# A decode layer's first weight load in two transfers, and x's transfers behind ScalarE's first function table

## The chip, the cores and the metric

The kernel runs on one core of one Trainium2 chip. The core has five engines with instruction queues of their own: PE (TensorE, matrix products), DVE (VectorE), ACT (ScalarE), POOL (GpSimd) and SP (SyncE, which here only issues transfers). Sixteen DMA engines move data between the device memory (HBM) and the core's on-chip memory (SBUF, 128 partitions). PE writes its results to a second memory, PSUM. The metric is the time of one execution in microseconds on the device; lower is better. A time that is given as a median is over runs without the profiler's page; the profile is of one further execution.

## The reference

One token of a transformer layer with attention and a gated feed-forward part side by side, all in float32:

```python
x = A_x                                   # 1 x 1 x 1024
xn = _layernorm(x, axis=-1)
return x + _A_ref(xn, A_k_cache, A_v_cache, A_wq, A_wo) + _B_ref(xn, B_w_gate, B_w_up, B_w_down)

# _A_ref: 32 query heads, 4 key heads, the last 4096 of 65536 cached positions, head size 128
q = (x @ wq)                              # wq 1024 x 4096
k, v = the last 4096 rows of k_cache, v_cache, each shared by 8 query heads
p = softmax(q k^T * 128 ** -0.5);  o = p v;  return o @ wo      # wo 4096 x 1024

# _B_ref
h = gelu(x @ w_gate) * (x @ w_up)         # 1024 x 3584 each
return h @ w_down                         # 3584 x 1024
```

With one token nearly all of the work is to read the weights and the cached window once: 94 MB.

## The kernel before, in words

Everything large goes through one buffer in SBUF, `ring`, of 128 partitions by 32768 float32 values. A list, `PLAN`, says in which order the pieces of weights and cache come, at which column of the ring each begins, and which earlier piece has to be used up before it may be loaded: two loads of wq (`("q", 0)` at column 0 and `("q", 1)` at 16384) may start at once, then keys and values of two pairs of heads, the two halves of w_gate, w_up, wo and w_down take their turns in the halves and quarters of the ring. `load` issues the transfers of one piece, all of them on SyncE's queue; `used` issues what waits for a piece, after the code that uses it. So SyncE's queue has the loads in the order of `PLAN`, and each waits there until its place in the ring is free.

The piece `("q", 0)` is 512 rows of wq, four rows to each partition: 64 KB, without a gap, in each of 128 partitions (partition p takes rows 4p to 4p + 3). Before the change `load` moves it in one transfer of 128 partitions. Keys are moved in two transfers of 64 partitions each, to the even and to the odd ones; all other pieces in transfers of 128 partitions.

The start of the program is in this order. ScalarE issues two transfers that bring x, cut into two rows of 512, to `x_rows` (one row a transfer), and two that bring x into `x_out`, which is added to the result at the end. VectorE clears or fills the constant tiles; one of them is `avg`, a tile of 128 x 128 values 1/1024. GpSimd makes `ident`, the identity. Then `used(None)` issues the two loads of wq on SyncE, which has nothing in front of them. `layer_norm` turns `x_rows` into columns with four transposes on PE, gets mean and variance with two products by `avg`, takes a square root on ScalarE (`AF.Sqrt`; right behind it a dummy `AF.Exp` of one column, so that the next function table is loaded early), and writes the normalized x to `xz`.

`project` multiplies a piece of weights with `xz`: of each partition's four rows, two go to PE (32 products of 128 x 512 for a piece of wq) and two to VectorE, which scales a row by a value for each partition and adds it to `part`; `projected` adds VectorE's part to PE's sum at the end. The work on a piece waits for the landing of all its transfers.

The order of all instructions is that of the program text. The class `Flow` records each instruction's reads and writes, builds the program twice, and in the second pass adds just those waits that the reads and writes ask for. All instructions pass through one line of `Flow.issue`, so the profile names line 208 for nearly everything, and groups are told apart by their tiles.

Of the kernel before, what the change touches and what calls it, by code (L numbers as in the profile page):

```python
# [5 lines left out]
F32 = mybir.dt.float32  # L6
AF = mybir.ActivationFunctionType
# [4 lines left out]
P = 128  # L12
D = 1024
# [5 lines left out]
NR = 4  # L19
NJ = D // (NR * P)  # L20
# [217 lines left out]
RING = 32768  # L238
# [11 lines left out]
def decode_layer(nc, x, k_cache, v_cache, wq, wo, w_gate, w_up, w_down, out):  # L250
    consts = stream = work = Pool(nc.nc, "sbuf")
    psum = Pool(nc.nc, "psum")

    def fours(w, jj):
        return w[NR * P * jj:NR * P * (jj + 1), :].rearrange("(p r) n -> p r n", r=NR)


    def windows(cache, i):
        pair = cache[0, 2 * i:2 * i + 2, SK - WIN:, :]
        return pair.rearrange("g (p j) d -> p g (j d)", p=P // 2)  # L260


    def grouped(w, start, rows):
        return w[start:start + P * rows, :].rearrange("(p t) n -> p t n", p=P)


    def sources(kind, i):
        if kind == "q":
            return [fours(wq, i)]
        if kind == "g":  # L270
            return [fours(w_gate, i)]
        if kind == "u":
            return [fours(w_up, i)]
        if kind == "ua":
            return [fours(w_up, i)[:, :2]]
        if kind == "ub":
            return [fours(w_up, i)[:, 2:]]
        if kind in "kv":
            cache = k_cache if kind == "k" else v_cache
            return [windows(cache, i)]  # L280
        if kind == "o":
            return [grouped(wo, P * WIDE * i, WIDE)]
        return [grouped(w_down, P * GROUP * i, min(GROUP, TD - GROUP * i))]

    ring = stream.tile([P, RING], F32, name="ring")
    loaded = {}

    def load(key, at):

        parts = {("d", 2): 2, ("d", 3): 4}.get(key, 1)  # L290
        first = at
        if key[0] in "kv":

            dst = ring[:, at:at + RING // 4]
            if key[0] == "v":
                nc.sync.dma_start(dst, sources(*key)[0])
            else:
                for odd in range(2):
                    nc.sync.dma_start(dst[odd:P:2], sources(*key)[0][:, odd])
            loaded[key] = ring[:, at:at + RING // 4]  # L300
            return
        for src in sources(*key):
            rows, n = src.shape[1:]
            dst = ring[:, at:at + rows * n].rearrange("p (t n) -> p t n", n=n)
            at += rows * n
            step = rows // parts
            for t in range(0, rows, step):
                cuts = 2 if key == ("d", 3) and t == rows - 1 else 1
                for cut in range(cuts):
                    cols = slice(cut * n // cuts, (cut + 1) * n // cuts)  # L310
                    nc.sync.dma_start(dst[:, t:t + step, cols], src[:, t:t + step, cols])
        loaded[key] = ring[:, first:at]

    def used(key):

        for new, at, old in PLAN:
            if old == key:
                load(new, at)


    x_rows = work.tile([NJ, NR * P], F32, name="x_rows")
    x_in = x.rearrange("a b (j p) -> (a b j) p", j=NJ)
    for j in range(NJ):
        nc.scalar.dma_start(x_rows[j:j + 1, :], x_in[j:j + 1, :])
    x_out = work.tile([P, CO], F32, name="x_out")
    nc.vector.memset(x_out, 0.0)
    x_in = x.rearrange("a b (h c n) -> (a b c) h n", h=2, c=4)
# [8 lines left out]
        out=ident, in_=ident, compare_op=ALU.not_equal, fill=1.0, base=0,  # L336
        pattern=[[-1, P]], channel_multiplier=1,
    )
    avg = consts.tile([P, P], F32, name="avg")
    nc.vector.memset(avg, 1.0 / D)  # L340

    xz = consts.tile([P, NR, NJ, 32], F32, name="xz")
    nc.vector.memset(xz, 0.0)
# [429 lines left out]
```

## Time and profile before

| | |
|---|---|
| median of 3 runs | 227.65 us (227.53 to 227.72) |
| profiled execution, its own time | 227.77 us |
| its span, first to last instruction | 225.9 us |
| busy: PE / DVE / ACT / POOL | 117.4 / 107.2 / 28.0 / 0.7 us |
| read from HBM | 94.38 MB, 418 GB/s over the span |
| issue to landing, two loads of wq | 21.9 and 40.8 us |

A row of the timeline gives the start in us, the duration in us, the engine, the line, the operation, the tile written `<-` the tiles read, the shape, and how many instructions it merges; in brackets stands how long the engine had been idle before it and what ended that. SPq and ACTq are the issuing of transfers on SyncE's and ScalarE's queues: the duration of such a row is that of issuing, not of moving data. "DMA to landing" is the time from an issue to the moment at which all of its data is there. In the windows, the DMA share is the mean busy share of the 16 DMA engines; a piece of a transfer is counted in the window in which it starts, so short windows can show more than 1. The chain of waits is followed back from the last instruction, at each step to what released it.

### The profile page before, as it was taken

What the parts mean: (1) busy time and instruction counts of PE and PEld (TensorE: products, weight loads), DVE (VectorE), ACT (ScalarE), POOL (GpSimd) and SP (SyncE); (2) the same over time, 40 slices, a digit from 0 to 9 for tenths busy, and PEclk for the clock granted to TensorE, in tenths of its full rate; (3) what the DMA queues carried; (4) which work ended last, traced back from release to release, by engine and by line L of the source; (5) the groups of instructions that cost most, each with busy time, mean ns of one, the idle gap of its engine ahead of it and who ended that gap; (6) DMA issues with size and microseconds to landing.
All of it is one profiled execution on the core that took longest, in us unless ns stands there. A gap on an engine that the chain in (4) does not pass through costs nothing.

```text
span 225.9 us, 2481 instructions
## 1 busy us (share of the span) xinstructions
PE 117.4 (52%) x1107; PEld 58.4 (26%) x1107; DVE 107.2 (47%) x129; ACT 28.0 (12%) x54; POOL 0.7 (0%) x6
## 2 busy tenths in 40 slices
PE   0120900558799861999844662135309905561756
PEld 0010200113655621755611110010004902220322
DVE  7030920591236082236059589149209705993801
ACT  2020000002435400455400310000000000000000
POOL 1000000000000000000000000000000000000000
PEclk9999995587999998599979958559956955855888
DMA  9899899899999999998999998999999999999992
GB/s 372 372 418 511 371 418 511 354 412 438 437 487 428 387 412 438 429 505 376 429 404 426 447 503 366 447 455 464 386 441 464 395 444 395 435 418 412 432 394 108
DMA packets 3242, 94.53 MB, mean 418 GB/s; under 512 B 398, under 2 KB 414, under 8 KB 1056
## 3 DMA queue, kind: packets, MB, share of 16 engines
q1 hardware_dynamic: 3208, 94.38, 97.4%
q8 instruction: 8, 0.13, 0.2%
q14 instruction: 2, 0.02, 0.0%
q10 hardware_dynamic: 24, 0.01, 0.0%
HBM read 94.38 MB, written 0.00 MB: 418 GB/s over the span
## 4 chain that ended last, share of the span: by engine, by line
DMA 80%; DVE 16%; PE 2%; issue 0%; SPq 0%; DVEq 0%
DMA ring<-in_B_w_gate 26%; DMA ring<-in_A_wq 18%; DVE part L208 14%; DMA ring<-in_A_wo 14%; DMA ring<-in_B_w_up 11%; DMA ring<-in_B_w_down 11%; DVE out_part L208 2%; PE out L208 2%; DVE y L208 0%; SPq L208 0%; DVE y_last L208 0%; DVEq L86 0%; DVE d L208 0%
## 5 line engine op out<-in xcount | busy, mean ns | idle before, releaser
L208 PE MATMUL acc<-ring,xz 128*32 128x512 f32 x176 | 31.7, 825 | 39.2 <-DMA ring<-in_A_wq 22.9
L208 DVE SCALAR_TENSOR_TENSOR part<-ring,xz,part 128x3584 f32<-128x3584 f32 (+1 forms) x9 | 37.2, 4128 | 21.8 <-DMA ring<-in_A_wq 12.5
L208 PE MATMUL tp<-ident,ring 128*128 128x128 f32 x128 | 20.6, 311 | 8.8 <-DMA ring<-in_A_k_cache 6.0
L208 DVE SCALAR_TENSOR_TENSOR out_part<-ring,oz,out_part 128x1024 f32<-128x1024 f32 x15 | 19.3, 1285 | 8.1 <-DMA ring<-in_A_wo 7.6
L208 PEld LDWEIGHTS acc<-ring,xz 128*32 128x32 f32 x176 | 7.1, 142 | 59.5 <-issue 25.2
L208 PE MATMUL out<-ring,hz 128*32 128x256 f32 (+1 forms) x160 | 13.9, 515 | 13.7 <-DMA ring<-in_B_w_down 13.7
L208 PE MATMUL out<-ring,oz 128*32 128x256 f32 x128 | 11.8, 551 | 17.3 <-DMA ring<-in_A_wo 17.3
L208 PEld LDWEIGHTS tp<-ident,ring 128*128 128x128 f32 x128 | 15.5, 156 | 16.9 <-DMA ring<-in_A_k_cache 6.9
L208 DVE COPY kT<-tp 128x512 f32<-128x512 f32 x12 | 8.1, 690 | 20.0 <-PE tp L208 20.0
L208 ACT ACTIVATE kT<-tp 128x512 f32<-128x512 f32 x20 | 11.4, 596 | 26.9 <-PE tp L208 26.9
L208 DVE TENSOR_SCALAR part<-ring,xz 128x3584 f32<-128x3584 f32 (+1 forms) x3 | 6.5, 2171 | 13.8 <-DMA ring<-in_A_wq 7.6
L208 DVE SCALAR_TENSOR_TENSOR out_part<-ring,hz,out_part 128x1024 f32<-128x1024 f32 x8 | 10.3, 1285 | 3.9 <-DMA ring<-in_B_w_down 3.6
L208 PEld LDWEIGHTS out<-ring,hz 128*32 128x32 f32 x160 | 6.1, 145 | 21.7 <-DMA ring<-in_B_w_down 16.1
L208 PE MATMUL acc<-part,units 128*32 128x512 f32 x44 | 7.2, 745 | 8.6 <-DVE part L208 8.6
L208 PEld LDWEIGHTS out<-ring,oz 128*32 128x32 f32 x128 | 5.3, 157 | 23.8 <-DMA ring<-in_A_wo 18.3
L208 PE MATMUL o<-ring,pT 128*32 128x128 f32 x256 | 8.0, 274 | 1.3 <-ACT pT L208 1.0
L208 DVE TENSOR_REDUCE m<-s 128x2 f32<-128x1024 f32 x4 | 4.9, 1224 | 6.1 <-PE s L208 6.1
L208 PE MATMUL s<-kT,qz 128*32 128x512 f32 x64 | 7.7, 598 | 0.0
L208 PEld LDWEIGHTS o<-ring,pT 128*32 128x32 f32 x256 | 6.8, 110 | 2.5 <-ACT pT L208 1.9
L208 PE MATMUL tp<-ident,x_rows 2*128 2x2 f32 x4 | 0.6, 252 | 10.4 <-DMA x_rows<-in_A_x 10.4
L208 PEld LDWEIGHTS tp<-ident,h_sb 128*64 128x64 f32 (+2 forms) x72 | 5.9, 229 | 0.4 <-issue 0.4
L208 PE MATMUL tp<-ident,h_sb 128*64 128x2 f32 (+2 forms) x72 | 6.0, 272 | 0.0
(88 smaller groups left out, 64.0 us busy)
## 6 DMA issues: line engine op xcount, KB each, us to landing
ring<-in_B_w_gate SPq DMA_DIRECT2D x2, 7168.0 KB, 29.5
ring<-in_A_k_cache SPq DMA_DIRECT2D x4, 2048.0 KB, 19.6
ring<-in_A_v_cache SPq DMA_DIRECT2D x2, 4096.0 KB, 26.8
ring<-in_B_w_down SPq DMA_DIRECT2D x2, 4096.0 KB, 26.5
ring<-in_B_w_up SPq DMA_DIRECT2D x2, 3584.0 KB, 21.5
ring<-in_B_w_up SPq DMA_DIRECT2D x1, 7168.0 KB, 26.0
ring<-in_B_w_down SPq DMA_DIRECT2D x2, 2048.0 KB, 22.7
ring<-in_B_w_down SPq DMA_DIRECT2D x3, 512.0 KB, 25.1
```

The source lines that it names most:

```text
L208: return lambda *a, **k: self.flow.issue(self.engine, lambda: call(*a, **k))
```

## The change

Three edits, all at the start of the program:

- `load` moves the piece `("q", 0)` in two transfers on SyncE's queue, the first to partitions 0 to 15, the second to partitions 16 to 127; before, it was one transfer to all 128.
- ScalarE's first instruction is now an activation with `AF.Sqrt` of one column of `avg` into a new tile `root` that nothing reads. Its function table is loaded in front of it, and ScalarE's transfers of x come behind it. To allow it, `avg` is filled before `x_out` is cleared on VectorE.
- x for the layer norm comes to `x_rows` in one transfer of two rows, not in two of one row.

The order of the instructions on PE stays the same; on VectorE only the two memsets change places; GpSimd's is the same.

```diff
@@ load
             loaded[key] = ring[:, at:at + RING // 4]
             return
+        if key == ("q", 0):
+            dst = ring[:, at:at + RING // 2].rearrange("p (t n) -> p t n", t=NR)
+            for some in (slice(0, 16), slice(16, P)):
+                nc.sync.dma_start(dst[some], sources(*key)[0][some])
+            loaded[key] = ring[:, at:at + RING // 2]
+            return
         for src in sources(*key):
@@ start of the program
     x_rows = work.tile([NJ, NR * P], F32, name="x_rows")
-    x_in = x.rearrange("a b (j p) -> (a b j) p", j=NJ)
-    for j in range(NJ):
-        nc.scalar.dma_start(x_rows[j:j + 1, :], x_in[j:j + 1, :])
+    avg = consts.tile([P, P], F32, name="avg")
+    nc.vector.memset(avg, 1.0 / D)
+    root = work.tile([P, 1], F32, name="root")
+    nc.scalar.activation(root, avg[:, 0:1], AF.Sqrt)
+    nc.scalar.dma_start(x_rows, x.rearrange("a b (j p) -> (a b j) p", j=NJ))
     x_out = work.tile([P, CO], F32, name="x_out")
     nc.vector.memset(x_out, 0.0)
...
-    avg = consts.tile([P, P], F32, name="avg")
-    nc.vector.memset(avg, 1.0 / D)
```

## The prediction

> **What bounds the kernel now.** I read the page first, then the chain of waits, then the timeline of the first 23 us. The page:
>
> ```profile
> span 225.9 us, 2481 instructions
> ...
> q1 hardware_dynamic: 3208, 94.38, 97.4%
> ...
> HBM read 94.38 MB, written 0.00 MB: 418 GB/s over the span
> ...
> DMA 80%; DVE 16%; PE 2%; issue 0%; SPq 0%; DVEq 0%
> ```
>
> SyncE's queue (q1) keeps 16 DMA engines busy for 97.4% of the span, and 80% of the chain that ended last is DMA. The rest of the chain lies beside further loads, as its pieces in order of time show:
>
> ```profile
> 50 pieces in order of time: start us, us, what
> ...
> 1.21 40.83 DMA ring<-in_A_wq
> ...
> 42.13 4.50 DVE part L208
> ...
> 46.65 4.50 DVE part L208
> ...
> 51.16 28.70 DMA ring<-in_B_w_gate
> ...
> 218.19 5.09 PE out L208 x64
> ```
>
> From the first landing on, every piece starts when something earlier in this chain ends. Whatever the first load loses or gains, all that follows moves by the same amount, since no engine has spare time in the stream of loads. What the first load itself costs is read from the start:
>
> ```profile
> 0.73 0.80 ACTq L208 DMA_DIRECT2D x_rows<-in_A_x  x2
> 0.73 0.89 SPq L208 DMA_DIRECT2D ring<-in_A_wq  x2
> 0.86 0.27 DVE L208 MEMSET x_out<- 128x256 f32 x1 [0.86 <-PEq L762]
> 1.11 0.17 DVE L208 MEMSET avg<- 128x128 f32 x1
> 1.57 0.57 ACTq L208 DMA_DIRECT2D x_out<-in_A_x  x2
> 2.17 1.28 ACT L208 ACT_TABLE_LOAD   x1 [2.17 <-issue]
> ...
> 10.36 0.61 PE L208 MATMUL tp<-ident,x_rows 2*128 2x2 f32 x4 [10.36 <-DMA x_rows<-in_A_x]
> ...
> 13.73 0.20 ACT L208 ACTIVATE st<-st 128x1 f32<-128x1 f32 x1 [10.28 <-DVE st L208]
> 13.95 1.28 ACT L208 ACT_TABLE_LOAD   x1
> ...
> 14.94 0.24 DVE L208 TENSOR_SCALAR xz<-xc,st 128x8 f32<-128x8 f32 x1
> ...
> 22.79 2.35 DVE L208 TENSOR_SCALAR part<-ring,xz 128x4096 f32<-128x4096 f32 x1 [7.61 <-DMA ring<-in_A_wq]
> 22.82 5.64 PE L208 MATMUL acc<-ring,xz 128*32 128x512 f32 x32 [9.32 <-DMA ring<-in_A_wq]
> ...
> 25.17 4.48 DVE L208 SCALAR_TENSOR_TENSOR part<-ring,xz,part 128x4096 f32<-128x4096 f32 x1
> ...
> 26.57 1.16 SPq L208 DMA_DIRECT2D ring<-in_A_k_cache  x2
> ```
>
> The layer norm is ready at 15.18 us (14.94 + 0.24), and VectorE then waits 7.61 us for the first load; so x is off the path, with 7.61 us to spare. Two loads' landings, counted from their issue, give the pace. The first answer is for the first load of wq (128 rows of 64 KB, 8192 KB), the second for both of its loads, the third and fourth for the first and for both of the first pair of key transfers (64 rows of 32 KB each, to every second partition):
>
> ```profile
> DMA to landing us min/median/max: 21.9/21.9/21.9
> ...
> DMA to landing us min/median/max: 21.9/31.4/40.8
> ...
> DMA to landing us min/median/max: 20.3/20.3/20.3
> ...
> L208 SPq DMA_DIRECT2D ring<-in_A_k_cache x2: 532/556/581, 26.6 to 27.2; - x2
> ...
> DMA to landing us min/median/max: 20.3/22.5/24.6
> ```
>
> Finally the windows; their last two columns are the DMA share and GB/s (a transfer's piece counts where it starts):
>
> ```profile
> core 0: us, PE busy (x) PEld busy (x) DVE busy (x) ACT busy (x) POOL busy (x), PEclk, DMA share, GB/s
> 1.50:2.60 1.10, 0.00 (x0) 0.00 (x0) 0.95 (x3) 0.43 (x1) 0.00 (x0) 1.00 2.83 955
> ...
> 22.00:40.00 18.00, 5.64 (x32) 1.39 (x32) 6.83 (x2) 0.00 (x0) 0.00 (x0) 0.83 1.00 433
> 43.00:51.00 8.00, 5.32 (x32) 1.12 (x24) 7.96 (x2) 0.00 (x0) 0.00 (x0) 0.71 0.98 422
> ```
>
> From 22 to 40 us 16 engines move 433 GB/s at a share of 1.00, 27.1 GB/s each: a row of 65,536 bytes takes an engine 2.42 us, and a load of 128 rows 8 such rounds, 19.3 us. In the first 1.1 us of data, 955 GB/s x 1.10 us is 16 rows, one for each engine, and 2.83 x 1.10 us says that these first rows took 3.11 us each, 0.69 us over the later ones.
>
> **The change part by part.** The sum is made against the profiled execution's own 227.77 us (span 225.9, so 1.87 us lie around it); the median shown is 227.65, 0.12 us below. The result is given against the median.
>
> *The first load in two.* It removes one issue on SyncE's queue and adds two, of 16 and of 112 rows. The extra issue is about 0.41 us (0.89 us for two in the row above). The second load of wq is issued that much later, but its rows wait behind the first load until about 22 us, and SyncE's next issue is at 26.57 us: nothing; without that cover 0.41 us. The readers of the first load wait for both transfers. Bytes and rows are the same. So the cost is only in the pace at which the rows are written, and this trace has no transfer to 16 neighbouring partitions. The even division is one row to each engine from the first transfer and seven from the second; which engine takes which row, no view shows.
>
> What caps the pace at 27.1 GB/s? It is the same for rows of 64 KB and, at 422 / 0.98 / 16 = 26.9, for the key rows of 32 KB: a hard ceiling. It may belong to the engine, or to the place written: 16 engines and 128 partitions are 16 groups of eight, and a path into such a group would give the same number if each engine always kept a path to itself. All wide loads, and the key loads too (2048 KB landing 51.8 - 46.9 = 4.9 us after the one before, 428 GB/s), spread over all 128 partitions, so the trace separates neither. The first transfer would: its 16 partitions are neighbours. Bounds: at the rate of the key loads, 2.42 us for the 16 rows (no cost); if eight neighbours have one path, two paths carry 16 rows in 8 rounds, 19.3 us. I take four paths, between the two (a path that serves four neighbours, and four more 32 further on): 4 rounds, 9.7 us, because a ceiling independent of row size on 16 groups fits a place at least as well as an engine. The Trainium skill, in SBUF — State Buffer, section "Door 1: The DMA port swizzle (why [64,N] ≈ [32,N])", states this rule outright: sixteen ports of eight partitions each, partitions 0 to 15 reach four, and 1 MiB to them was measured at 104 GB/s; by that price the first transfer takes 10.1 us, an estimate. No run here shows it yet; it is the rule that speaks against this change.
>
> The second transfer then matters as much. If each engine takes seven neighbours (rows 16 to 22, 23 to 29, ...), engines meet on the same path: the first has row 16 while the sixth has row 51 (16 + 32 + 3), one path in that rule. Stepping the sixteen engines through their seven rows, with each path shared equally between those who are on it, gives 11 rounds instead of 7, 26.6 us. Bounds: 7 rounds if the division avoids all meetings; 28 if the rows go out in sixteens (all four to a path each time). I take 11, as blocks are the plainest division. Then the second load of wq runs its 8 rounds as before. Sum: 4 + 11 + 8 = 23 rounds where there were 16, seven more at 2.42 us: 16.9 us. Does something hide it? DMA is what the chain waits for; PE (5.64 us) and VectorE (2.35 + 4.48 us) work through the first load beside the second, as before, and the key loads follow 26.57 - 22.79 = 3.8 us after its landing, still far ahead of the second landing. Nothing hides it.
>
> *A smaller first transfer may start sooner.* The first 16 rows start within 1.1 us and run 0.69 us long. A gain lies between 0 and that 0.69 us; a loss is bounded by the one more issue, 0.41 us. Without shared paths I take 0.3 us gain, nearer the middle; with them the first rows are slowed anyhow, and I take nothing.
>
> *ScalarE.* The table load (1.28 us) and a new one-column activation (0.20 us, as the row at 13.73) come first, and x's transfer, one for two, after them: its issue moves from 1.3 us at the latest to about 0.73 + 1.28 + 0.20 = 2.2 us. The activation waits for avg, which VectorE now sets first, at 0.86 + 0.17 us: before the table is there. Behind it on ScalarE's queue stand the two x_out issues (0.57 us), whose tile is needed at 223 us only; x_out's memset is 0.17 us later: nothing. x's landing was 9.1 us after its last issue, so now at 11.3 us, and one more row in front of it (2.42 us) makes 13.7; the layer norm takes 4.8 us more, 18.5 at the worst, under 22.79. The square root at 13.73 finds its table as before, and the second table load at 13.95 is off the path. Cost nothing, hidden by the first load; without the cover 1 to 3.4 us.
>
> **The rivals.** (a) *The ceiling is the engine's own.* Then 16 + 112 rows are 8 rounds as before and only the head start counts: 227.65 - 0.3 = 227.35, not slower. For it: key transfers of half the partitions run at full rate; against it: they reach every group, so they test nothing. It decides if the second load of wq still lands near 42 us. (b) *Only the first transfer is narrow*: the 112 rows keep the full pace, 3 rounds more, 7.3 us: 234.9. For it: 112 rows touch all groups. Against it: seven rows to an engine don't line up with groups of four. (c) *The 112 rows go out in sixteens*: 4 + 28 + 8 rounds, 24 more, 58 us: 285.7. Against it: the key loads, also 16 engines, would have met in the same way under such a division. (d) *x comes too late*, by some engine that holds its turn for a long slow row: needs over 7.6 us more, for which no row speaks, and the first load would be late with it; a few us at most, about 230. (e) The change of transfers does nothing and the start is as before: 227.65, part of (a).
>
> **How the numbers follow.** Forecast (paths shared, blocks of seven) 0.33: 227.65 + 16.9 = 244.6. (a) 0.30, of it 0.18 a gain above 0.2%, 0.12 within it. (b) 0.21, (c) 0.08, (d) and other small losses 0.08. 0.2% is 0.46 us, about what a measurement of this kernel tells from no change. Slower: 0.33 + 0.21 + 0.08 + 0.08 = 0.70. The likeliest case with (b) beside it, one mechanism, has its own range of 234 to 246; leaving out (a) would leave out too much, so the range reaches down to 227.1 (0.55 us of the 0.69 gained) and up to 246, with (c) outside.
>
> **What would show it.** Right: the window of the first data has 16 rows with a share that makes them near 9.7 us each; VectorE's first TENSOR_SCALAR on the ring starts near 39.7 us (22.79 + 16.9) and the second load of wq lands near 59; GB/s in between well under 433; from there on each row of the chain is 16.9 us later and equally long; x's MATMUL starts before 20 us. Wrong: the first TENSOR_SCALAR near 22.8 means (a); near 30 to 32, (b); near 80, (c). The forecast is most easily wrong in the number of paths and in how the 112 rows are dealt out, as both are taken and not read.

## The result, and the profile after

The changed kernel takes 249.11 us (median of 4 runs, 248.92 to 249.57) beside 227.62 us before: a ratio of 1.0945, 95% interval 1.0932 to 1.0957, or 21.5 us more. That is slower, as forecast, and by 4.6 us more than forecast. The time is also above the range, which ended at 246.

The profiled execution took 248.92 us at a span of 247.1. First the page of the changed kernel, the lines that answer to those of before:

```profile
span 247.1 us, 2482 instructions
...
q1 hardware_dynamic: 3224, 94.38, 97.1%
...
HBM read 94.38 MB, written 0.00 MB: 382 GB/s over the span
...
DMA 75%; DVE 19%; another core or an unknown queue 5%; issue 0%; SPq 0%; PE 0%; DVEq 0%
```

The bytes are the same and the DMA engines are busy for nearly the same share (97.1% for 97.4%) of a span that is 21.2 us longer: they don't idle, they move less while they are busy. The 5% that the chain puts down to an unknown queue are one wait, from 51.21 to 63.56 us, which the last row of the timeline puts down to the second load of wq. The timeline of the changed kernel says where the time goes:

```profile
0.73 1.31 SPq L208 DMA_DIRECT2D ring<-in_A_wq  x3
0.74 1.28 ACT L208 ACT_TABLE_LOAD   x1 [0.74 <-PEq L768]
1.04 0.55 ACTq L208 DMA_DIRECT2D x_rows<-in_A_x  x1
2.04 0.20 ACT L208 ACTIVATE root<-avg 128x1 f32<-128x1 f32 x1
12.87 0.61 PE L208 MATMUL tp<-ident,x_rows 2*128 2x2 f32 x4 [12.87 <-DMA x_rows<-in_A_x]
44.34 2.35 DVE L208 TENSOR_SCALAR part<-ring,xz 128x4096 f32<-128x4096 f32 x1 [26.65 <-DMA ring<-in_A_wq]
63.65 9.01 DVE L208 SCALAR_TENSOR_TENSOR part<-ring,xz,part 128x4096 f32<-128x4096 f32 x2 [12.44 <-DMA ring<-in_A_wq]
```

The first load is usable at 44.34 us where it was at 22.79: 21.55 us later. The second load of wq follows 19.3 us behind it (63.65 - 44.34), as before (42.13 - 22.79 = 19.3), and the end is 21.2 us later. So the whole loss is made before 44.34 us, and what follows neither gives it back nor adds to it by more than the 0.65 us by which the runs of this kernel differ among themselves.

In the windows a mean row can be read off: a row is 65,536 bytes on one of 16 engines, so it takes 1048.6 x (DMA share) / (GB/s) us. Each of the first eight windows holds the starts of one round of 16 rows (GB/s x length / 65,536 bytes is 16); the last lies in the second load of wq:

```profile
core 0: us, PE busy (x) PEld busy (x) DVE busy (x) ACT busy (x) POOL busy (x), PEclk, DMA share, GB/s
1.50:2.70 1.20, 0.00 (x0) 0.00 (x0) 0.95 (x3) 0.73 (x2) 0.00 (x0) 1.00 7.10 874
9.90:11.50 1.60, 0.00 (x0) 0.00 (x0) 0.00 (x0) 0.00 (x0) 0.00 (x0) 1.00 3.39 658
15.50:16.50 1.00, 0.52 (x2) 0.44 (x2) 0.17 (x2) 0.23 (x2) 0.00 (x0) 1.00 4.71 1050
20.00:22.00 2.00, 0.00 (x0) 0.00 (x0) 0.00 (x0) 0.00 (x0) 0.00 (x0) 1.00 1.63 525
23.00:26.00 3.00, 0.00 (x0) 0.00 (x0) 0.00 (x0) 0.00 (x0) 0.00 (x0) 1.00 1.27 350
27.00:30.00 3.00, 0.00 (x0) 0.00 (x0) 0.00 (x0) 0.00 (x0) 0.00 (x0) 1.00 1.47 350
31.00:34.00 3.00, 0.00 (x0) 0.00 (x0) 0.00 (x0) 0.00 (x0) 0.00 (x0) 1.00 1.56 350
35.90:39.00 3.10, 0.00 (x0) 0.00 (x0) 0.00 (x0) 0.00 (x0) 0.00 (x0) 1.00 1.47 338
44.50:60.00 15.50, 4.87 (x32) 1.12 (x27) 6.68 (x2) 0.00 (x0) 0.00 (x0) 0.81 0.96 414
```

The rows to partitions 0 to 15 take 8.52 us each. The seven rounds of the 112 rows take 5.40, 4.70, 3.26, 3.80, 4.40, 4.67 and 4.56 us, together 30.8. The second load of wq is back at 2.43 us. Sum of the eight means: 39.3 us, where before it was 3.11 + 7 x 2.42 = 20.0: 19.3 of the 21.55 us. The other 2.3 us are worked out only as the rest. The engines no longer stay together, and the landing waits for the last. This shows where they go on to the second load; its first 16 starts fit into 0.8 us before the change (first line) and need 2.9 us after it (second line):

```profile
21.60:22.40 0.80, 0.00 (x0) 0.00 (x0) 0.00 (x0) 0.00 (x0) 0.00 (x0) 1.00 3.04 1311
40.40:43.30 2.90, 0.00 (x0) 0.00 (x0) 0.00 (x0) 0.00 (x0) 0.00 (x0) 1.00 1.08 362
```

### The profile page after: what moved, and what is told of

The parts are those of the page before. It is cut to its first block, busy times and chain, and to the rows that moved or that the text cites. A ratio compares the mean times of both kernels' runs of the same rounds, so it can differ in the third digit from the quotient of the medians.

```text
span 247.1 us, 2482 instructions
## 1 busy us (share of the span) xinstructions
PE 115.5 (47%) x1107; PEld 57.2 (23%) x1107; DVE 107.2 (43%) x129; ACT 28.2 (11%) x55; POOL 0.7 (0%) x6
## 3 DMA queue, kind: packets, MB, share of 16 engines
q1 hardware_dynamic: 3224, 94.38, 97.1%
## 4 chain that ended last, share of the span: by engine, by line
DMA 75%; DVE 19%; another core or an unknown queue 5%; issue 0%; SPq 0%; PE 0%; DVEq 0%
DMA ring<-in_B_w_gate 24%; DMA ring<-in_A_wq 17%; DVE part L208 15%; DMA ring<-in_A_wo 12%; DMA ring<-in_B_w_up 11%; DMA ring<-in_B_w_down 10%; DVE out_part L208 3%; SPq L208 0%; PE tp L208 0%; DVE y_last L208 0%; DVEq L86 0%; DVE d L208 0%
## 5 line engine op out<-in xcount | busy, mean ns | idle before, releaser
L208 PE MATMUL acc<-ring,xz 128*32 128x512 f32 x176 | 32.6, 836 | 61.4 <-DMA ring<-in_A_wq 42.5
L208 DVE SCALAR_TENSOR_TENSOR out_part<-ring,oz,out_part 128x1024 f32<-128x1024 f32 x15 | 19.3, 1285 | 8.6 <-DMA ring<-in_A_wo 8.1
L208 DVE TENSOR_SCALAR part<-ring,xz 128x3584 f32<-128x3584 f32 (+1 forms) x3 | 6.5, 2172 | 32.8 <-DMA ring<-in_A_wq 26.6
L208 PE MATMUL out<-ring,hz 128*32 128x256 f32 (+1 forms) x160 | 13.7, 491 | 14.0 <-DMA ring<-in_B_w_down 14.0
L208 PEld LDWEIGHTS tp<-ident,ring 128*128 128x128 f32 x128 | 15.5, 156 | 16.3 <-DMA ring<-in_A_k_cache 7.0
L208 PE MATMUL out<-ring,oz 128*32 128x256 f32 x128 | 10.9, 514 | 17.8 <-DMA ring<-in_A_wo 17.8
L208 PEld LDWEIGHTS out<-ring,hz 128*32 128x32 f32 x160 | 5.4, 133 | 22.3 <-DMA ring<-in_B_w_down 18.3
L208 PE MATMUL acc<-part,units 128*32 128x512 f32 x44 | 5.8, 599 | 6.8 <-DVE part L208 6.8
L208 ACT ACTIVATE rows<-acc 128x1024 f32<-128x1024 f32 x1 | 1.0, 1023 | 56.7 <-PE acc L208 56.7
```

The lines of the kernel that those rows point to most:

```text
L208: return lambda *a, **k: self.flow.issue(self.engine, lambda: call(*a, **k))
```

## The experiments

The theory: the rate at which rows are written depends on which partitions are written at the same time, because groups of partitions share a path. The rivals: the two transfers cost something as such, or small ones do; rows that are neighbours in HBM are slow to read; x or the function table delays the start. The first experiment starts from the changed kernel, all others from the kernel before, with x and the table as they were. From the halves on, each is one run.

### The two parts alone

The first experiment keeps ScalarE's part and the reordered memsets, with the first load in one transfer as before:

```diff
-        if key == ("q", 0):
-            ...
-            for some in (slice(0, 16), slice(16, P)):
-                nc.sync.dma_start(dst[some], sources(*key)[0][some])
```

> ScalarE's part of the change alone (table first, x in one transfer behind it); the first load stays one transfer to 128 partitions. Theory (the places written share paths, so the loss is all in the split): about the time of the kernel before, 227.6 us, within 0.5 us, VectorE's first work on the ring near 22.8 us. Rival (x or the table delays the start): up to 249.

Measured: 227.68 us beside 227.68, ratio 1.0 (0.9991 to 1.0009). x now lands earlier, and it is worth nothing, as the timeline of this kernel shows:

```profile
7.98 0.61 PE L208 MATMUL tp<-ident,x_rows 2*128 2x2 f32 x4 [7.98 <-DMA x_rows<-in_A_x]
...
22.93 2.35 DVE L208 TENSOR_SCALAR part<-ring,xz 128x4096 f32<-128x4096 f32 x1 [10.12 <-DMA ring<-in_A_wq]
```

PE has x at 7.98 us, 2.38 us before the 10.36 of the kernel before, which is close to one row of 2.42 us. That the one transfer for x, in place of two, brings this is not shown: with two transfers as before, PE has x at 8.21 us in the run with even and odd partitions below, and beside the split at 12.80 us in the next run, where the changed kernel with its one transfer has it at 12.87. VectorE just waits longer for the ring: 10.12 us in place of 7.61.

The second keeps the split and leaves x and the table as before:

```diff
+            for some in (slice(0, 16), slice(16, P)):
+                nc.sync.dma_start(dst[some], sources(*key)[0][some])
...
     for j in range(NJ):
         nc.scalar.dma_start(x_rows[j:j + 1, :], x_in[j:j + 1, :])
```

> The split of the first load into 16 and 112 partitions alone, x as before. Theory: all of the loss, 249 us within 0.5 us, first work on the ring near 44.3 us. Rival (the two parts need each other): clearly less than 249.

Measured: 249.14 us, ratio 1.0948 (1.0932 to 1.0965), with the first work on the ring at 44.69 us. The split is all of it.

### Two transfers that divide the partitions otherwise

```diff
-            for some in (slice(0, 16), slice(16, P)):
+            for some in (slice(0, P, 2), slice(1, P, 2)):
```

> The first load in two transfers of 64 rows, to the even and to the odd partitions, as the keys are loaded. Theory (what counts is where the rows that are written at one time lie): no loss, 227.6 us within 0.5 us. Rival (a first load in two transfers costs by itself): well above, in the direction of 249.

Measured: 228.09 us, ratio 1.0018 (1.0009 to 1.0027). Two transfers cost 0.4 us, not 21.5. The window from 5 to 21 us of this kernel gives a row of 1048.6 x 1.06 / 459 = 2.42 us (below it, from the timeline, the products that wait for x):

```profile
5.00:21.00 16.00, 1.78 (x8) 1.56 (x8) 2.65 (x17) 1.69 (x3) 0.00 (x0) 1.00 1.06 459
...
8.21 0.61 PE L208 MATMUL tp<-ident,x_rows 2*128 2x2 f32 x4 [8.21 <-DMA x_rows<-in_A_x]
```

The same number of rows in each transfer, but in halves:

```diff
+            for some in (slice(0, 64), slice(64, P)):
```

> The first load in two transfers of 64 rows, to partitions 0 to 63 and to 64 to 127. Theory with rows dealt out in blocks of neighbours: every engine meets one other, on the path 32 partitions away, in all 8 rounds; rows near 4.65 us as in the fuller rounds after the change, 8 x 4.65 = 37.2 us for 19.3, so about 245.5 us. Theory with rows dealt out as pairs 16 apart (the only division that explains the keys' full rate by paths): four to a path, 8 x 8.5 = 68 us, about 276. Rival (rows that are neighbours in HBM are slow, not the places written): the rows of a round lie as far apart as in the load of 128, so 227.6.

Measured: 249.16 us. The window from 6.5 to 42 us:

```profile
6.50:42.00 35.50, 1.78 (x8) 1.55 (x8) 2.23 (x13) 1.69 (x3) 0.00 (x0) 1.00 1.01 207
```

The rate is 207 GB/s and a row takes 5.12 us, somewhat more than the 4.65 taken from the mixed rounds: hence 249 and not 245.5. Two engines to a path, as the theory has it for blocks; neither the full rate of the HBM rival nor the 276 of the other division. 64 rows reach the full rate or half of it by nothing but where they lie.

### Is it the place written, or the place read?

Here the 16 first partitions get pieces that lie far apart in HBM:

```diff
+            nc.sync.dma_start(dst[0:16], src[0:P:8])
+            nc.sync.dma_start(dst[16:P], src[16:P])
```

> As the split alone, but the first 16 partitions get every eighth partition's rows of wq (rows far apart in HBM) in place of their own, so part of the query projection uses wrong weights. Theory (the places written share paths): the first 16 rows take 8.5 us each as after the change, total 249. Rival (rows that are neighbours in HBM are slow to read): the first rows take near 3.1 us as before the change, total about 243.5.

And here sixteen neighbouring pieces of HBM go to every eighth partition, eight times:

```diff
+            for o in range(8):
+                nc.sync.dma_start(dst[o:P:8], src[16 * o:16 * o + 16])
```

> The first load in eight transfers of 16 rows; each reads 16 neighbouring pieces of HBM and writes them to every eighth partition (so rows of wq meet other rows of x than they should). Theory: two engines to a path, rows near 4.65 us, 8 x 4.65 = 37.2 us for 19.3, about 245.5. Rival (neighbours in HBM are slow): 8 rounds of 8.5 us, 68 us, about 276. Engine's own ceiling: 228 to 230.

Measured: 249.65 and 249.05 us. The first window of the first kernel has 1048.6 x 5.67 / 700 = 8.49 us a row, though what is read is spread:

```profile
1.50:3.00 1.50, 0.00 (x0) 0.00 (x0) 1.19 (x4) 0.83 (x1) 0.00 (x0) 1.00 5.67 700
```

The second has 5.12 us a row (share 1.01 at 207 GB/s from 6.5 to 42 us, as in the halves), though what is read are neighbours; by that the 245.5 us that were expected, with rows of 4.65, were too few. The next run reads the same pieces in the same order as this one and writes them to neighbours, at 9.36 us a row. The place read makes no difference; the place written does.

### Four to a path, eight times

```diff
+            for o in range(0, P, 16):
+                nc.sync.dma_start(dst[o:o + 16], sources(*key)[0][o:o + 16])
```

> The first load in eight transfers of 16 neighbouring partitions. Theory: the first round of the change eight times, 8 x 8.5 = 68 us for 19.3, about 276. If a full rate came back once the start is over (the slow first rows are a matter of the start): near 235.

Measured: 283.13 us, 55.3 more than the 227.81 run beside it. The rows do not recover; they even take a little longer than the first ones:

```profile
9.50:75.00 65.50, 1.78 (x8) 1.56 (x8) 2.23 (x13) 1.69 (x3) 0.00 (x0) 1.00 1.00 112
```

1.00 at 112 GB/s is 9.36 us a row, which is why 276 was too low by 7 us. Four paths at 28 GB/s each make these 112 GB/s; with two to a path it was 207 / 8 = 25.9 GB/s each, and 433 / 16 = 27.1 alone.

### Where 64 neighbours go at full rate

The rule taken in the prediction, four neighbours and the four 32 further on, says that the partitions 32 to 95 reach all sixteen paths, where 0 to 63 reach eight:

```diff
+            for some in (slice(32, 96), slice(0, 32), slice(96, P)):
+                nc.sync.dma_start(dst[some], src[some])
```

> The first load in three transfers: 64 rows to partitions 32 to 95, then 32 rows to 0 to 31 and 32 to 96 to 127. By the path rule (four neighbours and the four 32 further share a path) the middle 64 reach all sixteen paths, where 0 to 63 reach eight. Theory: the middle goes at full rate, 4 rounds of 2.42 us (the first 3.1), and each set of 32 has two engines to a path, 4 rounds of 5.1 us: 10.8 us over, about 238.4 us. Rival (contiguous or smaller transfers are slow as such, wherever they lie): the middle's rows take 5.1 us as in the halves, about 249.

Measured: 238.47 us against an expected 238.4. The windows of the 64 in the middle and of the 32s behind them:

```profile
5.00:11.00 6.00, 1.34 (x7) 1.20 (x7) 1.46 (x10) 0.00 (x0) 0.00 (x0) 1.00 1.21 525
...
16.70:31.00 14.30, 0.00 (x0) 0.00 (x0) 0.00 (x0) 0.00 (x0) 0.00 (x0) 1.00 1.06 220
```

2.42 us a row in the middle, 5.05 in the 32s. A contiguous transfer of 64 rows is at full rate or at half of it, as the rule says for each place.

### How the 112 rows are dealt out, and who is held up

Seven transfers of 16 rows, made so that each engine gets seven neighbours:

```diff
+            nc.sync.dma_start(dst[0:16], src[0:16])
+            for o in range(16, 23):
+                nc.sync.dma_start(dst[o:P:7], src[o:P:7])
```

> The 112 rows of the change dealt out by hand: after the 16 rows to partitions 0 to 15, seven transfers of 16 rows, each to every seventh partition from 16, 17, ... 22 on, so that each engine gets seven neighbours one after the other. Theory (a transfer of 112 is dealt out in such blocks): the same as after the change, 249 within 1 us, with the same mean row in each round (5.4, 4.7, 3.3, 3.8, 4.4, 4.7, 4.6 us). Rival (some other division): another time, by the fullest path of each round. If only the engines that meet are slowed, a mean row near 2.9 us in a round and about 243.

Measured: 249.3 us. Three of its rounds, to be held against those of the changed kernel that begin at 9.9, 15.5 and 31 us:

```profile
9.60:11.40 1.80, 0.00 (x0) 0.00 (x0) 0.00 (x0) 0.00 (x0) 0.00 (x0) 1.00 3.05 584
15.50:16.60 1.10, 0.27 (x2) 0.18 (x1) 0.48 (x3) 0.59 (x2) 0.00 (x0) 1.00 4.35 955
...
31.40:34.10 2.70, 0.00 (x0) 0.00 (x0) 0.00 (x0) 0.00 (x0) 0.00 (x0) 1.00 1.75 388
```

5.48, 4.78 and 4.73 us for 5.40, 4.70 and 4.67. A transfer of 112 rows behaves as if dealt out in blocks of seven. With that, the rows written in each round are known, and with the rule, who shares: in the first round the partitions 16, 23, 30, ... 121, of which only 16 with 51 and 72 with 107 share a path. Four of sixteen engines share, yet the mean row is 5.4 us, as if all did. A mean could also come from four very long rows, but further windows of the changed kernel exclude that. The engines are busy for 97.1% of the span, so one that is done starts its next row:

```profile
11.50:15.50 4.00, 1.26 (x7) 1.12 (x7) 1.04 (x6) 0.00 (x0) 0.00 (x0) 1.00 0.00 0
...
20.20:21.30 1.10, 0.00 (x0) 0.00 (x0) 0.00 (x0) 0.00 (x0) 0.00 (x0) 1.00 2.96 954
21.30:23.50 2.20, 0.00 (x0) 0.00 (x0) 0.00 (x0) 0.00 (x0) 0.00 (x0) 1.00 0.00 0
23.50:24.50 1.00, 0.00 (x0) 0.00 (x0) 0.00 (x0) 0.00 (x0) 0.00 (x0) 1.00 3.35 918
24.50:25.30 0.80, 0.00 (x0) 0.00 (x0) 0.00 (x0) 0.00 (x0) 0.00 (x0) 1.00 0.00 0
25.30:26.00 0.70, 0.00 (x0) 0.00 (x0) 0.00 (x0) 0.00 (x0) 0.00 (x0) 1.00 0.63 187
```

After the 16 starts from 9.9 to 11.5 us none follows before 15.5: none of the sixteen engines is done in less than 4.0 us. The third of the seven rounds, from 20.2 us on, is another matter: by the rule only one pair shares in it (88 with 123), and 14 engines are on to the next row by 24.5 us (918 GB/s x 1.00 us), the other two only after 25.3. Two pairs hold up all; in this round the one pair slows the others far less.

To see this from a round without any sharing on, the set was shifted:

```diff
+            for o in range(11, 18):
+                nc.sync.dma_start(dst[o:o + 106:7], src[o:o + 106:7])
+            for some in (slice(0, 11), slice(123, P)):
+                nc.sync.dma_start(dst[some], src[some])
```

> The first load in seven transfers of 16 rows, each to every seventh partition, from 11, 12, ... 17 on, and two small ones for partitions 0 to 10 and 123 to 127. Sixteen rows from 11 on all have paths of their own; from 12, 13, 14, 16 and 17 on two pairs share a path, from 15 on one pair. Theory (a shared path holds up all sixteen engines, not only the ones that share): first round 3.1 us as at any start, then mean rows of 4.5 to 5.4 us with two pairs and 3 to 4 us with one, though 12 to 14 of the 16 engines have a path alone. Rival (only those who share are slowed): means of 3.1 us with two pairs and 2.8 with one. Total about 249 by the theory, with the small transfers at four to a path.

Measured: 255.66 us. Its rounds from the first to the fifth, with no pair sharing, two, two, two, and one:

```profile
2.00:3.50 1.50, 0.00 (x0) 0.00 (x0) 1.33 (x2) 1.23 (x1) 0.00 (x0) 1.00 2.09 699
5.10:6.50 1.40, 0.19 (x2) 0.22 (x3) 0.32 (x4) 0.00 (x0) 0.00 (x0) 1.00 2.94 752
9.00:11.00 2.00, 0.46 (x2) 0.37 (x2) 1.06 (x7) 1.30 (x2) 0.00 (x0) 1.00 2.31 525
13.40:16.00 2.60, 0.00 (x0) 0.00 (x0) 0.00 (x0) 0.00 (x0) 0.00 (x0) 1.00 1.82 403
18.20:20.50 2.30, 0.00 (x0) 0.00 (x0) 0.00 (x0) 0.00 (x0) 0.00 (x0) 1.00 1.43 456
...
30.00:34.00 4.00, 0.00 (x0) 0.00 (x0) 0.00 (x0) 0.00 (x0) 0.00 (x0) 1.00 1.97 262
37.00:43.00 6.00, 0.00 (x0) 0.00 (x0) 0.00 (x0) 0.00 (x0) 0.00 (x0) 1.00 1.68 175
```

3.14 us without sharing, as at the start of the wide load (3.11); 4.10, 4.61 and 4.74 with two pairs; 3.29 with one. If only the four that share took two shares of 2.42, the mean would be about 3.0. So engines that have a path to themselves are held up too. The total was missed by 6.7 us at the end: with the 11 and the 5 last rows under way, rows take 7.88 and 10.07 us over two rounds, where one such round had been reckoned. These few rows again go to neighbouring partitions; the other 16 of the 32 that start in these two windows are already rows of the second load of wq.

No run beat the kernel before: ScalarE's part measures the same, and each other division of the first load was slower.

## Why the prediction was right in sign and too small in size

- *What bounds the kernel.* Right. A delay of 21.55 us in the first load's landing became 21.2 us at the end and 21.5 us in the median; the second load of wq lands 19.3 us behind the first as before, so nothing hid it.
- *Whose ceiling it is.* Right for the loss: it comes from the place written, not from the engine. Rival (a), no loss, is excluded by the 8.52 us rows; the two runs that changed source and destination separately show that it is the place. Four paths for partitions 0 to 15: right, 8.52 us for an expected 9.7 in the first round and 9.36 in the later ones of the run with eight sixteens. Here the Trainium skill's rule (SBUF — State Buffer, "Door 1: The DMA port swizzle (why [64,N] ≈ [32,N])") agrees with the trace but for a few per cent: it gives limits of about 109 GB/s for partitions 0 to 15 and 218 GB/s for 0 to 63, and 104 and 196 GB/s as measured with 1 MiB; 112 and 207 GB/s were measured here. The 112 lie above its limit, and the measurement decides. The middle 64 partitions, which the run put at full rate, follow from its table of ports. What caps an engine that has a path to itself at 27.1 GB/s stays open: a path with four engines carried 28.0.
- *How the 112 rows are dealt out.* Right, but by luck: the hand-made blocks of seven give the same rounds, but the reason given ("blocks are the plainest division") does not hold for the kernel before. Blocks of eight would write every eighth partition in each round of the load of 128, two engines to each path, and the run that does so took 5.12 us a row where that load took 2.42.
- *The step that failed* is "with each path shared equally between those who are on it, gives 11 rounds instead of 7, 26.6 us". The seven rounds took 30.8 us in their means. That step slowed only the engines that meet; measured, all sixteen were slowed in a round in which four of them met (none done in under 4.0 us). The number was also not what the step says: the seven rows alone, stepped in this way, give 9 rounds, 21.8 us (no engine shares in more than two of its seven rows). It comes to 11 if the engines that are done go on with the second load, each on one path, and meet those that are not, which the prediction doesn't say. Had each round been counted at its fullest path, as two shares, it would have been 14 rounds, 33.9 us, of which the measured 30.8 fall short mainly since the two rounds with a single pair are short (3.26 and 3.80 us). The sum then is 8.5 + 30.8 in place of 9.7 + 26.6, 3.0 us more, and 2.3 us put down to drift between the engines, which the prediction did not have, less the 0.7 us by which the first rows were long before the change too: 4.6 us in all.
- *A smaller first transfer may start sooner.* Nothing was taken, and nothing is seen: the first 16 rows begin between 1.5 and 2.7 us, before the change between 1.5 and 2.6.
- *ScalarE.* Cost nothing, right. But the transfer of x was not held until 2.2 us: its issue is at 1.04 us, while the table load runs from 0.74 to 2.02. The queue goes on issuing while the engine loads, so the transfer stood behind the table in the program only. PE had x at 12.87 us, behind first rows of 8.52 us. That this lies near the 13.7 reckoned is chance: the issue came 1.2 us sooner than reckoned, and the rows in front were far longer. VectorE still waited 26.65 us for the ring, which leaves nothing to rival (d).
- *Rivals (b) and (c).* (b), only the 16 rows slow, would have left rounds of 2.42 us from 9.9 us on; they are 3.3 to 5.4. (c) would have needed seven rounds of over 9 us, as the run with eight sixteens has them.

Open: the way in which engines with a path to themselves are held up, and why one pair does it far less than two. The Trainium skill describes something of the kind (DMA: Bandwidth & Descriptors, "Back-pressure in remote DMA": a saturated destination port clogs the path back, and other engines on that path with it); it says so of transfers between cores, and no run here shows the way back. Open too: why 64 rows to every second partition run at full rate. In blocks of four they would meet as the sets of every eighth partition did (5.12 us), and so would the load of 128 in blocks of eight; both must be dealt out in another manner than the 112, which no run here shows.

## What to carry to other kernels

Before you cut a load by partitions, list which partitions are written at the same time: here the load's rate followed the place written, from 433 GB/s over all 128 or over 32 to 95, to 207 over 0 to 63 and 112 over sixteen neighbours at a time. Which rows of a transfer go out together has to be tried, not assumed: it was blocks for 112 rows and something else for 128. A load that keeps all sixteen DMA engines "busy" can still run at a quarter of its rate, so read GB/s beside the share. And where a resource is shared unevenly, reckon also with the case that all wait for the fullest part, not only those on it: here the seven rounds took as long as 12.7 at full rate (30.8 / 2.42), for 11 forecast.

## What the runs showed of the hardware that was not expected

Two pairs of engines that share a path hold up all sixteen: mean rows of 4.1 to 5.4 us with two pairs, 3.3 to 3.8 with one, where in the first such round two engines alone are late, 2.42 with none once the start is over. A path's total was a little lower with two sharers (25.9 GB/s) and a little higher with four (28.0) than alone (27.1), each from one run and from rounded shares. ScalarE's queue issues a transfer while the table load before it in the program is still running (1.04 us against 0.74 to 2.02).
